# A decode layer (windowed attention plus MLP on one token): the last weight's second half loaded in three pieces, a filler matmul, and two constants made by another engine

## The chip, the cores and the metric

The kernel runs on one core of one Trainium2 chip. A core has five engines that work side by side: TensorE (PE, matmuls), VectorE (DVE), ScalarE (ACT), GpSimd (POOL) and SyncE (SP, which here only issues loads and the store), and 16 DMA engines that move data between the chip's memory (HBM) and the on-chip memory (SBUF). Matmul results go to PSUM. The metric is the device time of one execution in microseconds; the time given for a kernel is the median of its runs.

## The reference, cut to what matters

One token `x` of 1024 values is normalized; the result goes through attention over the last 4096 positions of a cache (32 query heads, 4 key/value heads, head size 128) and through an MLP, and both results are added to `x`. All inputs are bf16.

```python
xn = _layernorm(x)
# attention
q = (xn @ wq) as 32 heads of 128                 # wq 1024 x 4096
k, v = the last W = 4096 rows of k_cache, v_cache, each of 4 heads serves 8 query heads
p = softmax(q k^T * 128 ** -0.5)
A = (p v) as one row of 4096 @ wo                # wo 4096 x 1024
# MLP
h = gelu(_layernorm(xn) @ w1 + b1)               # w1 1024 x 3584
B = h @ w2 + b2                                  # w2 3584 x 1024
out = x + A + B
```

## The kernel before, in words

Every weight is used once, for one token, so the kernel is a stream of loads with the arithmetic hung beside it. In bytes: K 4 MiB, wq 8, w1 7, V 4, w2 7, wo 8.

**Loads.** SP issues nearly all of them in this order: K in four pieces (L76), wq in two halves (L85), half of b1 (L204), w1 (L207), V in four pieces (L214), w2 (L220), wo's first half, wo0, in one piece and its second half, wo1, in four (L228). A weight is laid over 128 partitions so that partition p holds consecutive rows of it; for wo, one of the two halves has 16 row groups per partition, called rows here (row r of wo1 is `tv[:, r, :]`, 128 x 1024 values, 256 KiB). ScalarE issues four small loads after its first activation (L108 to L111): x as 32 x 32 (`x32`), x and b2 as 4 x 256 each (`xb8`), and half of b1. Buffers are reused: wo1 lies where V was, so its issue waits until V has been read (L302); w2 lies where the transposed K was.

**Constants.** GpSimd makes them at the start: the zero block `zb` and identity `ident`, `zf` (512 zero columns `zeros`, the mask `sel4`, and two columns `sel01`, L112 to L120), `o8z` (128 x 32 x 3, zero, L115/L116), selection masks (L125 to L134) and `gmask`. `sel01` is a 33 x 2 matrix whose only 1 stands in row 0, column 1. ScalarE makes `ident_f`, the identity in fp32 (L96).

**Start.** `x32` is spread over the 128 partitions by four matmuls (L145), normalized twice (`layernorm`, ScalarE, TensorE and GpSimd), giving `xnT` for wq and `yT` for w1. VectorE transposes K in blocks (L191); VectorE and ScalarE move the blocks into place (L200, L202).

**Middle.** q (L237), the first MLP product (L249), scores (L266), softmax, p v (L302), and the attention row written to column 1 of `o8z` (L313), so that `o8z[:, c, 1:2]` is the vector for row c of wo, and `o8z[:, c, 0:2]` and `o8z[:, c, 1:3]` are that vector beside a zero column.

**End.** `chunk_src` lists 60 rows: 28 of w2, 16 of wo0, 16 of wo1. The first `n_bulk` = 52 (w2, wo0 and wo1's rows 0 to 7) go through two 512-column matmuls each into `accf` (L329), which had x and b2 added to it at the start (L184). Before the first row of wo0, two fp32 matmuls with zero operands clear the tail's accumulators `acct` (L326); they stand behind the last matmul of w2 by `tc.issue_after`. ScalarE copies `accf` to `bulk` (L333). The last `TAIL` = 8 rows take another way: eight short matmuls each (120 or 136 columns, L348), four side by side in the array, into the two `acct` tiles. At `idx == 0`, ahead of the first tail row, six fp32 matmuls (twelve instructions in the trace, L342) add the columns of `bulk` to the same tiles; one of their selection matrices is `sel01`. VectorE adds the rest of `bulk` while it takes the first tile (L351), ScalarE takes the second (L352), and SP and ScalarE store two rows each (L354, L355).

The order on each engine is made at build time by the framework from the order of the source, the data and its own estimate of times; `tc.issue_after(ins)` holds what is in its block behind `ins` on that engine.

Of the kernel before, what the change touches and what calls it, by code (L numbers as in the profile page):

```python
# [7 lines left out]
FP32 = mybir.dt.float32  # L8
BF16 = mybir.dt.bfloat16
ACT = mybir.ActivationFunctionType  # L10
ALU = mybir.AluOpType
# [4 lines left out]
def kernel(  # L16
# [14 lines left out]
    nc = tc.nc  # L31
    P = 128
# [13 lines left out]
    CW2 = Fd // P  # L46
    CWO = NQ // P
# [10 lines left out]
    ps_tp = ctx.enter_context(tc.tile_pool(name="ps_tp", bufs=1, space=bass.MemoryType.PSUM))  # L58
# [4 lines left out]
    def ring_tile(name):  # L63
        return ring.tile([P, RING_ELEMS], BF16, tag="ring", name=name, align_bytes=256)
# [4 lines left out]
    x_flat = A_x.rearrange("a b d -> (a b d)")  # L69
# [12 lines left out]
    for i in range(2):  # L82
# [11 lines left out]
                            pattern=[[-1, P]], channel_multiplier=1)  # L94
    ident_f = consts.tile([P, P], FP32)
# [7 lines left out]
    x32 = consts.tile([32, 32], BF16)  # L103
# [1 line left out]
    b1_8 = consts.tile([8, NH], BF16)  # L105
    b1_v = B_b1.rearrange("(a n) -> a n", a=8)
    with tc.issue_after(first_exp.ins):
        nc.scalar.dma_start(out=x32[:], in_=x_flat.rearrange("(a n) -> a n", a=32))  # L108
        nc.scalar.dma_start(out=xb8[0:4, :], in_=x_flat.rearrange("(a n) -> a n", a=4))
        nc.scalar.dma_start(out=xb8[4:8, :], in_=B_b2.rearrange("(a n) -> a n", a=4))  # L110
        nc.scalar.dma_start(out=b1_8[0:4, :], in_=b1_v[0:4, :])  # L111
    zf = consts.tile([P, 512 + Hq + 2], FP32)  # L112
    nc.gpsimd.memset(zf[:], 0.0)
    zeros = zf[:, 0:512]
    o8z = consts.tile([P, CWO, 3], BF16)  # L115
    nc.gpsimd.memset(o8z[:], 0.0)  # L116
    sel4 = zf[:, 512:512 + Hq]
    sel01 = zf[0:33, 512 + Hq:]
    nc.gpsimd.affine_select(out=sel01, in_=sel01, compare_op=ALU.not_equal, fill=1.0, base=-1,
                            pattern=[[1, 2]], channel_multiplier=2)  # L120
    qm_f = zb[:, P:P + 160]
    spread = zb[0:Hq, 288:800].rearrange("h (q p) -> h q p", q=4)
    sel_b = zb[0:8, 800:1056].rearrange("k (s m) -> k s m", s=2)
# [1 line left out]
    for sel, base in ((sel_x, 0), (sel_x, -64), (sel_b, 0)):  # L125
        nc.gpsimd.affine_select(out=sel, in_=sel, compare_op=ALU.not_equal, fill=1.0, base=base,
                                pattern=[[-16, 2], [-1, sel.shape[2]]], channel_multiplier=16)
    for R in range(4):
        nc.gpsimd.affine_select(out=sel4, in_=sel4, compare_op=ALU.not_equal, fill=1.0, base=-32 * R,
                                pattern=[[-1, Hq]], channel_multiplier=1)  # L130
# [3 lines left out]
                            pattern=[[-1, 4], [1, P]], channel_multiplier=-4)  # L134
# [4 lines left out]
                            pattern=[[-REP, Hkv]], channel_multiplier=1)  # L139
    nc.gpsimd.affine_select(out=gmask[:], in_=gmask[:], compare_op=ALU.is_ge, fill=0.0, base=REP - 1,  # L140
                            pattern=[[REP, Hkv]], channel_multiplier=-1)
# [38 lines left out]
    acch = ps_acc.tile([P, 2, 512], FP32, tag="acch", name="acch")  # L180
    for b in range(2):
        nc.scalar.copy(out=accq[:, b, :], in_=zeros)
    for s in range(2):
        nc.tensor.matmul(accf[0:64, 256 * s:256 * s + 256], lhsT=sel_x[:, s, :], rhs=xb8[:], start=(s == 0), stop=False)  # L184

# [34 lines left out]
    nc.sync.dma_start(out=w2v, in_=w2_v)  # L220
    chunk_src += [("h", r, w2v[:, r, :]) for r in range(CW2)]
    wo_v = A_wo.rearrange("(p c) n -> p c n", p=P)
    for i, cuts in enumerate([[0, 16], [0, 8, 13, 15, 16]]):
        nr = CWO // 2
        t = ring_tile(f"wo{i}")
        tv = t[:].rearrange("p (r n) -> p r n", r=nr)
        for a, b in zip(cuts[:-1], cuts[1:]):
            nc.sync.dma_start(out=tv[:, a:b, :], in_=wo_v[:, nr * i + a:nr * i + b, :])  # L228
        chunk_src += [("o", nr * i + r, tv[:, r, :]) for r in range(nr)]


    for i, w3 in enumerate(wq_tiles):
        for r in range(4):
            c = 4 * i + r
            for j in range(NJQ):
                b, t = divmod(j, 4)
                nc.tensor.matmul(accq[32 * t:32 * t + 1, b, :], lhsT=xnT[:, c:c + 1], rhs=w3[:, r, j * 512:(j + 1) * 512],  # L237
                                 start=(c == 0), stop=(c == C - 1), tile_position=(0, 32 * t))
# [6 lines left out]
    for c in range(C):  # L245
        for b in range(2):
            for t in range(4):
                j = 2 * t + b
                nc.tensor.matmul(acch[32 * t:32 * t + 1, b, :NH], lhsT=yT[:, c:c + 1], rhs=w1v[:, c, j * NH:(j + 1) * NH],  # L249
                                 start=False, stop=(c == C - 1), tile_position=(0, 32 * t))  # L250
# [11 lines left out]
    for a in range(WQ4 // 512):  # L262
        for R in range(4):
            for g in range(Hkv):
                c0 = WQ4 * R + 512 * a
                nc.tensor.matmul(sp[32 * R:32 * R + 32, a, :], lhsT=qm[:, g, :], rhs=kT[:, g, c0:c0 + 512],  # L266
                                 start=(g == 0), stop=(g == Hkv - 1), tile_position=(0, 32 * R))
# [33 lines left out]
    for c in range(NCH):  # L301
        nc.tensor.matmul(o_all[:].rearrange("h g d -> h (g d)"), lhsT=eTb[:, 32 * c:32 * c + 32], rhs=v4[:, :, c, :],  # L302
                         start=(c == 0), stop=(c == NCH - 1))
# [18 lines left out]
    for idx, (kind, c, wap) in enumerate(chunk_src[:n_bulk]):  # L322
        if idx == CW2:
            with tc.issue_after(last.ins):
                for i, (t, n) in enumerate(zip(acct, widths)):
                    nc.tensor.matmul(t[64 * i:64 * i + 34, :], lhsT=zeros[:, 0:34], rhs=zeros[:, 0:n], start=True, stop=False,  # L326
                                     tile_position=(0, 64 * i))
        for half in range(2):
            last = nc.tensor.matmul(accf[32 * half:32 * half + 1, :], lhsT=vec[kind](c),  # L329
                                    rhs=wap[:, half * 512:(half + 1) * 512],  # L330
                                    start=False, stop=(idx == n_bulk - 1), tile_position=(0, 32 * half))
# [4 lines left out]
    parts = [(i, r, half) for r in range(2) for i in range(2) for half in range(2)]  # L336
    cols = ((0, NE), (NE, 256))
    for idx, (kind, c, wap) in enumerate(chunk_src[n_bulk:]):
        if idx == 0:
            for i, r, half in [(1, 0, 0), (1, 0, 1), (0, 1, 0), (0, 1, 1), (1, 1, 0), (1, 1, 1)]:  # L340
                g0 = 64 * i + 32 * half
                nc.tensor.matmul(acct[i][g0:g0 + 2, :], lhsT=row_sel[(half, r)],  # L342
                                 rhs=bulk[0:33, 256 * r + cols[i][0]:256 * r + cols[i][1]],
                                 start=False, stop=False, tile_position=(0, g0))
        for i, r, half in parts:
            g0 = 64 * i + 32 * half
            w0 = 512 * half + 256 * r
            nc.tensor.matmul(acct[i][g0:g0 + 2, :], lhsT=o8z[:, c, 1 - r:3 - r], rhs=wap[:, w0 + cols[i][0]:w0 + cols[i][1]],  # L348
                             start=False, stop=(idx == TAIL - 1 and r == 1), tile_position=(0, g0))
# [36 lines left out]
```

## Time and profile before

| | us |
|---|---|
| median of 3 runs (101.68 to 101.92) | 101.8 |
| the profiled execution, its own time | 101.61 |
| its span, first to last instruction | 99.5 |
| PE busy | 47.6 |
| VectorE busy | 37.5 |
| ScalarE busy | 28.9 |
| GpSimd busy | 8.9 |
| bytes read from HBM | 39.86 MB |
| rate over the span | 401 GB/s |

A page of the profile gives busy time per engine, groups of instructions with what ended the idle time before them (written `[idle <-releaser]`), the chain of work that ended last, and the loads. A timeline line reads: start, duration, engine, source line, operation, tile written `<-` tiles read, shapes, count, idle time and releaser; `SPq` and `ACTq` are the issuing of loads by those engines. A line of a stretch reads: its length, then busy time and count for PE, its weight loads, VectorE, ScalarE and GpSimd, then the granted TensorE clock (1.00 is full), the DMA engines' mean busy share, and GB/s. The busy shares of 48% and less show that no engine is full over the whole span; the loads are at 94% (the queue of SP's and the other ordinary loads, as a share of the 16 DMA engines' time).

### The profile page before, as it was taken

What the parts mean: (1) busy time and instruction counts of PE and PEld (TensorE: products, weight loads), DVE (VectorE), ACT (ScalarE), POOL (GpSimd) and SP (SyncE); (2) the same over time, 40 slices, a digit from 0 to 9 for tenths busy, and PEclk for the clock granted to TensorE, in tenths of its full rate; (3) what the DMA queues carried; (4) which work ended last, traced back from release to release, by engine and by line L of the source; (5) the groups of instructions that cost most, each with busy time, mean ns of one, the idle gap of its engine ahead of it and who ended that gap; (6) DMA issues with size and microseconds to landing.
All of it is one profiled execution on the core that took longest, in us unless ns stands there. A gap on an engine that the chain in (4) does not pass through costs nothing.

```text
span 99.5 us, 1001 instructions
## 1 busy us (share of the span) xinstructions
PE 47.6 (48%) x405; PEld 20.2 (20%) x405; DVE 37.5 (38%) x25; ACT 28.9 (29%) x32; POOL 8.9 (9%) x35
## 2 busy tenths in 40 slices
PE   0005110007600880089139807999100999895770
PEld 0003110002100310063036402334000333341240
DVE  0079999999999970010613015000600000000001
ACT  5306200007999999900150080000010000000201
POOL 7921560000000000000001000000000000000000
PEclk9999999999999999999999985579955558999999
DMA  2999999999999888999499999899899999899930
GB/s 46 389 409 435 484 428 474 474 422 422 448 422 581 369 369 369 392 669 415 181 425 422 435 576 392 369 576 491 369 392 418 422 422 422 362 441 408 394 114 1
DMA packets 2539, 39.91 MB, mean 401 GB/s; under 512 B 340, under 2 KB 360, under 8 KB 616
## 3 DMA queue, kind: packets, MB, share of 16 engines
q1 hardware_dynamic: 2460, 39.85, 93.9%
q8 instruction: 3, 0.05, 0.2%
q10 hardware_dynamic: 76, 0.01, 0.1%
HBM read 39.86 MB, written 0.00 MB: 401 GB/s over the span
## 4 chain that ended last, share of the span: by engine, by line
DMA 79%; PE 14%; SPq 3%; issue 1%; DVE 0%; DVEq 0%
DMA v_sb<-in_A_v_cache_dram 32%; DMA wo<-in_A_wo_dram 25%; DMA kq<-in_A_wq_dram 17%; PE o_all L302 10%; DMA kq<-in_A_k_cache_dram 5%; PE accq L237 4%; SPq L214 1%; SPq L228 1%; SPq L207 0%; PE acct L348 0%; DVE res L351 0%; DVEq L351 0%
## 5 line engine op out<-in xcount | busy, mean ns | idle before, releaser
L200 ACT COPY kt<-kt 32x4096 bf16<-32x4096 bf16 x5 | 18.0, 3601 | 10.2 <-DVE kt L191 10.2
L191 DVE STREAM_TRANSPOSE kt<-kq 128x4096 bf16<-128x4096 bf16 x4 | 17.4, 4413 | 5.6 <-DMA kq<-in_A_k_cache_dram 5.6
L202 DVE COPY kt<-kt 32x4096 bf16<-32x4096 bf16 x11 | 13.4, 1218 | 0.2
L302 PE MATMUL o_all<-v_sb,w1t 128*32 128x512 bf16 x32 | 9.8, 480 | 3.4 <-DMA v_sb<-in_A_v_cache_dram 3.4
L329 PE MATMUL accf<-w2t 128*1 128x512 bf16 x56 | 8.9, 496 | 4.8 <-DMA w2t<-in_B_w_dram 4.8
L351 DVE TENSOR_TENSOR res<-acct,bulk 34x120 bf16<-34x120 f32 x1 | 0.3, 275 | 25.1 <-PE acct L348 25.1
L237 PE MATMUL accq<-kq,xnT 128*1 128x512 bf16 x32 | 3.6, 625 | 10.2 <-DMA kq<-in_A_wq_dram 10.2
L333 ACT COPY bulk<-accf 34x512 f32<-34x512 f32 x1 | 0.6, 579 | 20.9 <-PE accf L329 20.9
L237 PE MATMUL accq<-wq,xnT 128*1 128x512 bf16 x32 | 3.6, 627 | 6.1 <-DMA wq<-in_A_wq_dram 6.1
L329 PE MATMUL accf<-wo,o8z 128*1 128x512 bf16 x48 | 5.5, 379 | 1.6 <-DMA wo<-in_A_wo_dram 1.6
L237 PEld LDWEIGHTS <-xnT 128*1 128x1 bf16 x64 | 2.1, 115 | 20.6 <-issue 20.6
L302 PEld LDWEIGHTS <-w1t 128*32 128x32 bf16 x32 | 3.7, 117 | 9.4 <-issue 7.4
L329 PEld LDWEIGHTS <-w2t 128*1 128x1 bf16 x56 | 3.0, 103 | 10.3 <-issue 8.6
L249 PE MATMUL acch<-w1t,yT 128*1 128x448 bf16 x64 | 5.1, 488 | 0.0
L305 DVE TENSOR_TENSOR o_m<-o_all,grs 32x512 f32<-32x512 f32 x1 | 0.7, 679 | 9.1 <-PE o_all L302 9.1
L297 DVE STREAM_TRANSPOSE w2t<-w1t 128x896 bf16<-128x896 bf16 x1 | 1.7, 1702 | 6.2 <-ACT w1t L294 6.2
L145 PE MATMUL x_ps<-x,zb 32*128 32x8 bf16 x4 | 0.2, 163 | 7.9 <-DMA x<-in_A_x_dram 7.9
L309 ACT CAST o_bf<-o_f 32x128 bf16<-32x128 f32 x1 | 0.3, 297 | 12.6 <-DVE o_f L307 12.6
L266 PE MATMUL sp<-kt,zb 128*32 128x512 bf16 x32 | 3.7, 631 | 0.3 <-DVE zb L258 0.3
L253 PE MATMUL qT_ps<-zb,w1t 128*128 128x128 bf16 x8 | 1.0, 311 | 5.2 <-ACT w1t L239 5.2
L293 POOL TENSOR_SCALAR zcol<-l_loc 128x1 f32<-128x1 f32 x1 | 0.2, 238 | 36.9 <-ACT w1t L281 36.9
L249 PEld LDWEIGHTS <-yT 128*1 128x1 bf16 x64 | 3.1, 108 | 1.5
(80 smaller groups left out, 40.6 us busy)
## 6 DMA issues: line engine op xcount, KB each, us to landing
w1t<-in_B_w_dram SPq DMA_DIRECT2D x1, 7168.0 KB, 24.0
w2t<-in_B_w_dram SPq DMA_DIRECT2D x1, 7168.0 KB, 29.8
kq<-in_A_k_cache_dram SPq DMA_DIRECT2D x4, 1024.0 KB, 7.1
kq<-in_A_wq_dram SPq DMA_DIRECT2D x1, 4096.0 KB, 17.2
wq<-in_A_wq_dram SPq DMA_DIRECT2D x1, 4096.0 KB, 24.3
v_sb<-in_A_v_cache_dram SPq DMA_DIRECT2D x4, 1024.0 KB, 25.9
wo<-in_A_wo_dram SPq DMA_DIRECT2D x1, 4096.0 KB, 39.1
wo<-in_A_wo_dram SPq DMA_DIRECT2D x1, 2048.0 KB
```

Of the source, the lines that this page charges most:

```text
L191: nc.vector.transpose(out=scr[:, g, :], in_=k2[:, g, :])
L200: nc.scalar.copy(out=dst, in_=src)
L202: nc.vector.tensor_copy(out=dst, in_=src)
L214: nc.sync.dma_start(out=v4[:, g, :, :], in_=A_v_cache[0, g, Sk - W:Sk, :].rearrange("(p c) d -> p c d", p=P))
L228: nc.sync.dma_start(out=tv[:, a:b, :], in_=wo_v[:, nr * i + a:nr * i + b, :])
L237: nc.tensor.matmul(accq[32 * t:32 * t + 1, b, :], lhsT=xnT[:, c:c + 1], rhs=w3[:, r, j * 512:(j + 1) * 512], start=(c == 0), stop=(c == C ...
L249: nc.tensor.matmul(acch[32 * t:32 * t + 1, b, :NH], lhsT=yT[:, c:c + 1], rhs=w1v[:, c, j * NH:(j + 1) * NH], start=False, stop=(c == C - 1 ...
L253: nc.tensor.transpose(qT_ps[:, b * 4 + hh, :], q_sb[:, b, hh * Dh:(hh + 1) * Dh], ident)
L266: nc.tensor.matmul(sp[32 * R:32 * R + 32, a, :], lhsT=qm[:, g, :], rhs=kT[:, g, c0:c0 + 512], start=(g == 0), stop=(g == Hkv - 1), tile_po ...
L297: nc.vector.transpose(out=hT, in_=h_sb.rearrange("p (d c) -> p c d", c=CW2))
L302: nc.tensor.matmul(o_all[:].rearrange("h g d -> h (g d)"), lhsT=eTb[:, 32 * c:32 * c + 32], rhs=v4[:, :, c, :], start=(c == 0), stop=(c == ...
L329: last = nc.tensor.matmul(accf[32 * half:32 * half + 1, :], lhsT=vec[kind](c), rhs=wap[:, half * 512:(half + 1) * 512], start=False, stop= ...
```

## The change

Five edits:

- wo1 is loaded in pieces of 9, 6 and 1 rows, no longer 8, 5, 2 and 1.
- Before the first row of wo1 (`idx == CW2 + CWO // 2`, row index 44) a filler matmul is issued behind the last matmul of wo0: fp32 zeros, 33 columns of weights, 512 moving columns, into a PSUM tile that nobody reads.
- The six matmuls that add `bulk` come before the second tail row, no longer before the first; so wo1's row 8 comes ahead of them.
- `sel01` and `o8z` are no longer made by GpSimd (a masked select and a memset). ScalarE copies one column of `ident_f` into `sel01`'s second column and zeros into `o8z`.
- `x32` is loaded by two loads of 16 partitions each, no longer by one of 32.

```diff
     with tc.issue_after(first_exp.ins):
-        nc.scalar.dma_start(out=x32[:], in_=x_flat.rearrange("(a n) -> a n", a=32))
+        for a0 in (0, 16):
+            nc.scalar.dma_start(out=x32[a0:a0 + 16, :], in_=x_flat.rearrange("(a n) -> a n", a=32)[a0:a0 + 16, :])
...
     o8z = consts.tile([P, CWO, 3], BF16)
-    nc.gpsimd.memset(o8z[:], 0.0)
     sel4 = zf[:, 512:512 + Hq]
     sel01 = zf[0:33, 512 + Hq:]
-    nc.gpsimd.affine_select(out=sel01, in_=sel01, compare_op=ALU.not_equal, fill=1.0, base=-1,
-                            pattern=[[1, 2]], channel_multiplier=2)
...
     for b in range(2):
         nc.scalar.copy(out=accq[:, b, :], in_=zeros)
+    nc.scalar.copy(out=sel01[:, 1:2], in_=ident_f[0:33, 0:1])
+    nc.scalar.copy(out=o8z[:].rearrange("p c f -> p (c f)"), in_=zeros[:, 0:3 * CWO])
...
-    for i, cuts in enumerate([[0, 16], [0, 8, 13, 15, 16]]):
+    for i, cuts in enumerate([[0, 16], [0, 9, 15, 16]]):
...
+        if idx == CW2 + CWO // 2:
+            with tc.issue_after(last.ins):
+                fill = ps_tp.tile([P, 512], FP32, tag="tp", name="fill")
+                nc.tensor.matmul(fill[0:33, :], lhsT=zeros[:, 0:33], rhs=zeros, start=True, stop=True)
         for half in range(2):
             last = nc.tensor.matmul(accf[32 * half:32 * half + 1, :], lhsT=vec[kind](c),
...
     for idx, (kind, c, wap) in enumerate(chunk_src[n_bulk:]):
-        if idx == 0:
+        if idx == 1:
             for i, r, half in [(1, 0, 0), (1, 0, 1), (0, 1, 0), (0, 1, 1), (1, 1, 0), (1, 1, 1)]:
```

## The prediction

> **What bounds the kernel now.** I read the chain of waits first: does an engine or the load stream set the end?
>
> ```profile
> DMA 79%; PE 14%; SPq 3%; issue 1%; DVE 0%; DVEq 0%
> DMA v_sb<-in_A_v_cache_dram 32%; DMA wo<-in_A_wo_dram 25%; DMA kq<-in_A_wq_dram 17%; PE o_all L302 10%; DMA kq<-in_A_k_cache_dram 5%; PE accq L237 4%; SPq L214 1%; SPq L228 1%; SPq L207 0%; PE acct L348 0%; DVE res L351 0%; DVEq L351 0%
> ```
>
> The stream does: 79% of the span is loads, and 39.9 MB at a mean of 401 GB/s fill 99.5 us. Pieces in which PE or SP stands in the chain (o_all L302, SPq L228) lie in front of loads that still had others ahead of them, so they are no price. The timeline of PE at the end shows what each piece of wo's second half (wo1) costs:
>
> ```profile
> 89.73 0.81 PE L329 MATMUL accf<-wo,o8z 128*1 128x512 bf16 x6
> 91.77 1.89 PE L329 MATMUL accf<-wo,o8z 128*1 128x512 bf16 x16 [1.23 <-DMA wo<-in_A_wo_dram]
> ...
> 94.89 0.76 PE L348 MATMUL acct<-wo,o8z 128*2 128x120 bf16 x40
> 96.04 0.41 PE L348 MATMUL acct<-wo,o8z 128*2 128x120 bf16 x16 [0.38 <-DMA wo<-in_A_wo_dram]
> 96.65 0.29 PE L348 MATMUL acct<-wo,o8z 128*2 128x120 bf16 x8 [0.20 <-DMA wo<-in_A_wo_dram]
> ```
>
> PE waits for wo1's rows 0 to 7 until 91.77, for rows 13 and 14 until 96.04, for row 15 until 96.65; wo's first half started at 86.92. So eight rows take 4.85 us (0.606 each), seven rows in two pieces 4.27, the last 0.61. Behind the last landing stand 0.29 us of PE, 0.28 of VectorE and the store.
>
> Then the stream's own end, in quarter microseconds (the last two columns are the DMA engines' busy share and GB/s):
>
> ```profile
> 95.00:95.25 0.25, 0.25 (x26) 0.25 (x22) 0.00 (x0) 0.00 (x0) 0.00 (x0) 1.00 0.41 156
> 95.25:95.50 0.25, 0.25 (x28) 0.21 (x15) 0.00 (x0) 0.00 (x0) 0.00 (x0) 1.00 0.12 49
> 95.50:95.75 0.25, 0.16 (x10) 0.00 (x0) 0.00 (x0) 0.00 (x0) 0.00 (x0) 1.00 0.11 41
> ```
>
> 0.12 of 16 is two engines: the last microsecond belongs to two that lag. The page gives instruction fetches three packets and 0.2% of the engines' time, 0.002 x 16 x 99.5 / 3 = 1.1 us each, and two of them fall inside the stream (between 48.5 and 50, and 69 and 70.2 us), so I read one fetch on each laggard. The change adds no PE work before 90 us that would shift those two.
>
> Last, the clock, in stretches between the moments at which the granted clock changes (PE busy is the second number, the clock the third from the end):
>
> ```profile
> 55.55:58.96 3.41, 1.35 (x28) 0.71 (x20) 0.00 (x0) 1.94 (x2) 0.00 (x0) 1.00 1.46 625
> ...
> 69.20:72.60 3.40, 1.10 (x8) 0.50 (x7) 1.68 (x2) 0.35 (x2) 0.00 (x0) 1.00 1.06 455
> ...
> 89.67:93.08 3.41, 2.18 (x24) 0.79 (x20) 0.00 (x0) 0.00 (x0) 0.00 (x0) 1.00 0.94 399
> 93.08:96.50 3.42, 2.31 (x74) 1.16 (x71) 0.00 (x0) 0.58 (x1) 0.00 (x0) 1.00 0.63 249
> ```
>
> The changes (near 58.96, 65.78, 72.6, 82.84) lie whole multiples of 3.41 us apart. Stretches with PE busy 1.35 us (40%) and 1.10 us (32%) were followed by half clock; 2.18 (64%) and 2.31 (68%) were not. The limit lies between 40% and 64%.
>
> **The change, part by part.**
>
> *Pieces 8, 5, 2, 1 become 9, 6, 1.* One load less. With r per row and d per piece, 8r + d = 4.85 and r + d = 0.61 give d below 0.01 us; 8r + d = 4.85 and 7r + 2d = 4.27 give 0.02. The far bound: V comes in four pieces. From 32.59 (wq's second half) to 60.29 (V) is 27.70 us for w1 and V; w2, as large as w1, takes 77.27 - 60.29 = 16.98; so V takes 10.72, against 32.59 - 22.91 = 9.68 for the same bytes in one piece: 0.35 us for each of three more. That stretch holds a fetch of about 1 us, which explains it nearly whole, so I take d = 0.01 and keep 0.35. The issues (four, 1.75 us from 70.09) have wo's first half still ahead until 86.92; one of 0.43 us less saves nothing.
>
> Landings: nine rows at 91.77 + 0.61 = 92.38, rows 9 to 14 at 96.03, row 15 at 96.64. PE's work behind 96.03 grows from 24 matmuls to 56. Rate: 40 in 0.76 us, the last one 0.218 (median of L348), is (0.76 - 0.218)/39 = 13.9 ns from start to start. 56 of them end at 96.03 + 55 x 0.0139 + 0.218 = 97.01, and row 15 is in place before its turn (48 x 0.0139 = 0.67, at 96.70). Before: 96.65 + 0.29 = 96.94. So **+0.07 us**. The upper bound is the 16-group's 0.41/16 = 25.6 ns: 96.03 + 1.43 = 97.46, +0.52. I take 13.9, the longest uninterrupted group.
>
> *Row 8 ahead of the six selections of bulk.* The 16 bulk matmuls run 92.38 to 94.27 (1.89), row 8 another 0.11; ScalarE's copy to 94.89 (0.04 + 0.58), the twelve matmuls of L342 from 94.95 for 0.6 (94.34 to 94.96 now) to 95.55. The next work waits for 96.03. Cost 0; 0.48 us of cover. If the order stayed as it was, the same cover would hold it.
>
> *Filler.* L326 clears 120 and 136 columns in fp32 in 0.43 us; 512 columns are 0.86 us by that if its positions run in turn, 1.6 if side by side, 0.21 if fp32 cost as much as one 512-column bf16 matmul (two started per 0.21 in wo). From 90.54 (89.73 + 0.81) it ends between 90.75 and 92.2, before 92.38 in all cases: 0. What it buys is busy time: 89.67 to 93.08 would hold 0.87 + 0.86 + 0.70 = 2.43 us (71%), without it 1.57 (46%), inside the open interval. The poorest 3.41 us, from the filler's end at 91.40, hold 92.38 to 94.38 = 2.0 (59%); before, from 90.54, 1.89 (55%).
>
> [...]
>
> *Start.* These lines show the cover:
>
> ```profile
> 7.93 0.24 PE L145 MATMUL x_ps<-x,zb 32*128 32x8 bf16 x4 [7.93 <-DMA x<-in_A_x_dram]
> ...
> 22.91 3.58 PE L237 MATMUL accq<-kq,xnT 128*1 128x512 bf16 x32 [10.22 <-DMA kq<-in_A_wq_dram]
> ...
> 23.11 7.22 ACT L200 COPY kt<-kt 32x4096 bf16<-32x4096 bf16 x2 [10.20 <-DVE kt L191]
> ```
>
> GpSimd loses 0.17 (o8z) and 0.18 us (sel01) and its last mask comes earlier, but x_ps waits for x, not for it: 0. ScalarE gains two copies; bounds 0.17 (smallest activation) and 0.30 (L309), together under 0.6, beside 10.20 us idle: 0. The second x load adds an issue of 0.38 us (L108), so x may be complete at 8.3; xn is ready near 12.2 and wanted at 22.91: 0. If that cover were gone, it would cost those 0.4 us.
>
> [...]
>
> One thing moves with the extra load. wq's halves and b1 are issued at 5.64, 8.29 and 10.71, when K's pieces 0, 1 and 2 have landed: each waits for the eighth load before it. With one more ahead, the ScalarE-issued half of b1 waits for piece 0 (behind it the accf copy, 4.13 to about 5.7; ScalarE's next work is at 8.21), and wq's halves for pieces 1 and 2, at 8.29 and 10.71. K's last bytes are then still coming: piece 3 lands near 10.71 + 2.42 = 13.1, and a load needs about 4.83 - 2.42 = 2.4 us from issue to its first byte, so wq's first bytes are there at 10.7: some 2 us of cover. Past it, every microsecond is one at the end.
>
> **Sum.** +0.07 against the profiled execution's own 101.61 us (span 99.5 and 2.1 around it): 101.68. The median of the runs is 101.80, 0.19 higher; on it, **101.87**. A difference under 0.2% (0.2 us) can't be told from none, so my forecast is no difference, with its own range 101.67 to 102.0.
>
> **Rivals.**
>
> 1. A piece costs more than two landings show. At 0.35 us the sum is -0.35 + 0.08 = -0.27: 101.53. For it: V's time. Against: the one-row piece at 0.61. [...] 0.12.
> 2. Some of the runs shown already lose the clock at the end. The stretch at 55% is inside the open interval, and an execution whose 3.41 us steps fall there runs the last work at half clock: bulk's selections 0.62 more, the 40 about 0.55 more, less 0.58 idle, then 0.1 to 0.3 on the last rows, some 0.4 us at most. The filler raises that stretch to 59%. Worth about 0.25 on the median: 101.55. Against: the runs spread by 0.24 only. 0.10.
> 3. **Slower: the clock falls in front of the last 56 matmuls.** If the filler (on zeros) doesn't count as busy, the stretch to 93.08 holds 46%; if the limit is above that, PE gets half clock from there to the end: 96.03 + 55 x 0.0278 + 0.3 = 97.86 instead of 96.94, +0.9: 102.7. Against: nothing shows that it doesn't count. 0.13.
> 4. Slower: the long group starts at the 16-group's pace, +0.5: 102.3. Against: the 40-group at 13.9. 0.11.
> 5. Slower: the stream starves when wq waits for a later piece of K, or a fetch moves; 0.4 to 1.0. Against: 2 us of cover. 0.08.
> 6. The order written isn't the order built (row 8 behind the selections): no change to the sum; it is within the forecast.
>
> **How the numbers follow.** No difference 0.46; faster 0.12 + 0.10 = 0.22; slower 0.13 + 0.11 + 0.08 = 0.32. The range takes in rivals 1, 2 and 4, from 101.48 to 102.4; outside are rival 3, part of 5 and little else, under 0.2.
>
> **What would show it.** In the timeline after: PE's waits for wo end near 92.4 and 96.0 and none ends at row 15 (one group of 56 of about 0.98 us); filler done before 92.2; granted clock 1.00 from 83 us to the end; L342 over before 96; SP's first wq issue near 8.3. Wrong is the forecast if the last landing moves by over 0.2 us, if the group of 56 takes over 1.2 us, or if the clock drops after 90 us.

## The result, and the profile after

The changed kernel takes 101.47 us (median of 14 runs, 101.30 to 101.80) against 101.84 us (14 runs, 101.68 to 101.96): ratio 0.9968, 95% interval 0.9958 to 0.9978. It is faster by 0.3%, a small difference but clear of the noise. The forecast was 101.87 and no difference, with a range of 101.48 to 102.4 that takes in three of the rivals.

The profiled execution of the changed kernel took 101.56 us, and its span is 99.8 us, *longer* than the 99.5 of before. So the gain is not in the span. First the two lines of its chain of waits:

```profile
DMA 80%; PE 13%; SPq 2%; issue 1%; DVE 0%; DVEq 0%
DMA v_sb<-in_A_v_cache_dram 32%; DMA wo<-in_A_wo_dram 27%; DMA kq<-in_A_wq_dram 14%; PE o_all L302 9%; DMA kq<-in_A_k_cache_dram 7%; PE accq L237 4%; SPq L214 1%; PE acct L352 1%; SPq L76 0%; SPq L207 0%; SPq L228 0%; DVE res L355 0%; DVEq L355 0%
```

The stream of loads sets the span as before. The timeline of PE at the end (L331 is the filler, L333, L346 and L352 were L329, L342 and L348):

```profile
87.16 3.62 PE L333 MATMUL accf<-wo,o8z 128*1 128x512 bf16 x32 [1.21 <-DMA wo<-in_A_wo_dram]
90.70 1.05 PE L331 MATMUL fill<-zf 128*33 128x512 f32 x2
92.59 1.46 PE L333 MATMUL accf<-wo,o8z 128*1 128x512 bf16 x12 [0.84 <-DMA wo<-in_A_wo_dram]
...
94.31 0.27 PE L352 MATMUL acct<-wo,o8z 128*2 128x120 bf16 x4
95.15 0.28 PE L346 MATMUL acct<-bulk,ident_f 33*2 33x136 f32 x2 [0.57 <-ACT bulk L337]
...
96.23 1.00 PE L352 MATMUL acct<-wo,o8z 128*2 128x120 bf16 x56 [0.45 <-DMA wo<-in_A_wo_dram]
```

Nine rows arrive 5.43 us after wo0 started (92.59 - 87.16), six more 3.64 us later: 0.60 to 0.61 us per row again. The filler is over at 91.75, the selections start at 95.15 and are done half a microsecond ahead of 96.23, and one group of 56 takes 1.00 us.

The last microsecond again has a DMA share of two engines or less (stretches of a quarter microsecond, columns as before):

```profile
95.25:95.50 0.25, 0.25 (x11) 0.18 (x5) 0.00 (x0) 0.00 (x0) 0.00 (x0) 1.00 0.12 49
95.50:95.75 0.25, 0.25 (x8) 0.04 (x1) 0.00 (x0) 0.00 (x0) 0.00 (x0) 1.00 0.04 16
95.75:96.00 0.25, 0.03 (x2) 0.04 (x1) 0.00 (x0) 0.00 (x0) 0.00 (x0) 1.00 0.13 49
```

The clock at the end, in stretches between this execution's own steps of 3.41 us (its clock changes at 71.12, 81.36 and 98.43):

```profile
88.19:91.60 3.41, 3.41 (x26) 1.02 (x22) 0.00 (x0) 0.00 (x0) 0.00 (x0) 1.00 0.96 411
91.60:95.01 3.41, 2.15 (x25) 0.88 (x24) 0.00 (x0) 0.49 (x1) 0.00 (x0) 1.00 0.94 392
95.01:98.43 3.42, 1.63 (x68) 1.16 (x68) 0.28 (x1) 0.36 (x2) 0.00 (x0) 1.00 0.06 22
```

The clock is full up to 98.43, past the last matmul (96.23 + 1.00), with PE busy 100%, 63% and 48%; it halves after the last of these. At the start, the timeline shows the moved work under its cover:

```profile
8.20 0.24 PE L143 MATMUL x_ps<-x,zb 32*128 32x8 bf16 x4 [8.20 <-DMA x<-in_A_x_dram]
...
8.29 0.33 SPq L85 DMA_DIRECT2D kq<-in_A_wq_dram  x1
...
23.05 3.60 ACT L200 COPY kt<-kt 32x4096 bf16<-32x4096 bf16 x1 [9.88 <-DVE kt L191]
```

x_ps is 0.27 us later, wq's first half is issued at 8.29 in place of 5.64, ScalarE still idles 9.88 us. None of this reaches the end.

Where, then, is the gain? Time less span is 101.61 - 99.5 = 2.11 us before and 101.56 - 99.8 = 1.76 after. The record of the granted clock runs on behind the last instruction; a stretch of the profile shows half clock to the end of that record and 1.00 behind it. Before:

```profile
101.00:102.00 1.00, 0.00 (x0) 0.00 (x0) 0.00 (x0) 0.00 (x0) 0.00 (x0) 0.54 0.00 0
```

After:

```profile
101.00:102.00 1.00, 0.00 (x0) 0.00 (x0) 0.00 (x0) 0.00 (x0) 0.00 (x0) 0.57 0.00 0
```

0.54 is half clock for 0.92 us and 0.57 for 0.86, so the record ends at 101.92 and at 101.86, in both 0.3 us past the execution's own time (101.61, 101.56). In all 20 profiled executions of this document that distance is 0.30 or 0.31 us, which suggests that what lies in front of the span is the same in all. What is left between the last instruction and that end is 2.4 us before and 2.1 after. The 0.35 us sit *behind* the last recorded instruction.

### The profile page after: what moved, and what is told of

Read it like the earlier page. It is cut to its first block, busy times and chain, and to the rows that moved or that the text cites. A ratio compares the mean times of both kernels' runs of the same rounds, so it can differ in the third digit from the quotient of the medians.

```text
span 99.8 us, 1004 instructions
## 1 busy us (share of the span) xinstructions
PE 47.3 (47%) x407; PEld 20.3 (20%) x407; DVE 37.5 (38%) x25; ACT 29.1 (29%) x34; POOL 8.6 (9%) x33
## 4 chain that ended last, share of the span: by engine, by line
DMA 80%; PE 13%; SPq 2%; issue 1%; DVE 0%; DVEq 0%
DMA v_sb<-in_A_v_cache_dram 32%; DMA wo<-in_A_wo_dram 27%; DMA kq<-in_A_wq_dram 14%; PE o_all L302 9%; DMA kq<-in_A_k_cache_dram 7%; PE accq L237 4%; SPq L214 1%; PE acct L352 1%; SPq L76 0%; SPq L207 0%; SPq L228 0%; DVE res L355 0%; DVEq L355 0%
## 5 line engine op out<-in xcount | busy, mean ns | idle before, releaser
L333 PE MATMUL accf<-w2t 128*1 128x512 bf16 x56 | 8.1, 460 | 6.0 <-DMA w2t<-in_B_w_dram 6.0
L302 PE MATMUL o_all<-v_sb,w1t 128*32 128x512 bf16 x32 | 8.8, 443 | 2.6 <-DMA v_sb<-in_A_v_cache_dram 2.6
L333 PE MATMUL accf<-wo,o8z 128*1 128x512 bf16 x48 | 5.5, 379 | 2.0 <-DMA wo<-in_A_wo_dram 2.0
L249 PE MATMUL acch<-w1t,yT 128*1 128x448 bf16 x64 | 6.2, 574 | 0.0
L333 PEld LDWEIGHTS <-w2t 128*1 128x1 bf16 x56 | 2.8, 97 | 10.9 <-issue 8.6
L249 PEld LDWEIGHTS <-yT 128*1 128x1 bf16 x64 | 3.6, 122 | 1.8
```

## The experiments

The reading in all of them is the time, the ratio to the kernel before, and time less span. "Length" is the number of instructions that the trace records for GpSimd, with its semaphore and register instructions; it is 60 before and 57 after. The expectations of e7 to e10 count the entries of GpSimd's list as it is built, which are fewer: 40 before, 38 after. Spans are given to 0.1 us, so a single time less span is good to 0.05.

| run | what it is | length | time, us | ratio [95%] | time less span, median (range) |
|---|---|---|---|---|---|
| e0 | before, unchanged | 60 | 101.74 | 0.999 [0.998, 1.000] | 2.12 (2.05 to 2.24) |
| e1 | x in two loads | 60 | 101.93 | 1.0001 [0.9992, 1.0010] | 2.14 (2.09 to 2.22) |
| e2 | constants on ScalarE | 57 | 101.47 | 0.9966 [0.9955, 0.9977] | 1.79 (1.68 to 1.90) |
| e3 | pieces, filler, order | 60 | 101.83 | 0.9994 [0.9984, 1.0004] | 2.12 (2.07 to 2.26) |
| after | all | 57 | 101.47 | 0.9968 [0.9958, 0.9978] | 1.72 (1.67 to 1.88) |
| e4 | o8z alone moved | 59 | 101.70 | 0.9992 [0.9980, 1.0004] | 1.99 (1.92 to 2.02) |
| e5 | sel01 alone moved | 58 | 101.45 | 0.9967 [0.9949, 0.9986] | 1.75 (1.70 to 1.79) |
| e6 | both on VectorE | 57 | 101.43 | 0.9956 [0.9945, 0.9967] | 1.78 (1.71 to 1.87) |
| e7 | e2 and 3 idle clears | 60 | 101.86 | 1.0012 [1.0000, 1.0023] | 2.14 (2.08 to 2.25) |
| e8 | before and 3 idle clears | 63 | 101.56 | 0.9969 [0.9959, 0.9979] | 1.86 (1.84 to 1.90) |
| e9 | before and 9 | 69 | 101.92 | 1.0013 [1.0003, 1.0023] | 1.78 (1.74 to 1.89), span 100.1 |
| e10 | after, 3 clears more off GpSimd | 54 | 101.45 | 0.9964 [0.9950, 0.9978] | 1.76 (1.74 to 1.87) |
| e11 | after without filler | 57 | 101.54 | 0.9976 [0.9966, 0.9986] | 1.77 (1.68 to 1.85) |
| e12 | before and 24 | 84 | 101.39 | 0.9964 [0.9952, 0.9975] | 1.71 (1.68 to 1.86) |
| e13 | before and 60 | 120 | 101.46 | 0.9965 [0.9953, 0.9977] | 1.76 (1.67 to 1.84) |
| e14 | before and 32 | 92 | 101.38 | 0.9955 [0.9936, 0.9975] | 1.73 (1.68 to 1.78) |
| e15 | before and 64 | 124 | 101.47 | 0.9969 [0.9953, 0.9984] | 1.73 (1.67 to 1.77) |
| e16 | before and 128 | 188 | 101.78 | 0.9990 [0.9963, 1.0017] | 2.05 (2.00 to 2.09) |
| e17 | before and 137 | 197 | 101.91 (one run) | | 1.81, span 100.1 |

### Which edit: e0 to e3

e0 is the kernel before with a comment line. e1 has only this edit:

```diff
-        nc.scalar.dma_start(out=x32[:], in_=x_flat.rearrange("(a n) -> a n", a=32))
+        for a0 in (0, 16):
+            nc.scalar.dma_start(out=x32[a0:a0 + 16, :], in_=x_flat.rearrange("(a n) -> a n", a=32)[a0:a0 + 16, :])
```

e2 has only the edits of `o8z` and `sel01`, e3 only the pieces, the filler and `idx == 1`, each as in the diff of the change.

> The kernel before, unchanged (a comment line is added), to learn how its time and its span stand to each other over many executions. In the profiled executions the time less the span is 2.11 us before and 1.76 us after (1.67 to 1.88 over 14). Theory A (the gain lies outside the span): time less span is near 2.1 in nearly all executions here, and spans are near 99.7, no longer than those of the changed kernel. Theory B (the profiled execution of before was one with a short span by chance, and the gain is in the stream of loads): time less span is near 1.75 here too, and spans are near 100.1. Ratio to before 1.000 within 0.001 by both.

> Only the x load in two halves. Theory A1 (this edit makes the gain, through the order of waits of the first loads): ratio near 0.997, time less span near 1.75. Theory A2 (another edit does): ratio 1.000, time less span near 2.1. Theory B (stream's end): ratio 1.000, since the end is untouched. By all: SP issues wq's first half near 8.3 us, no longer 5.6, and x_ps starts near 8.2.

> Only the two constants moved from GpSimd to ScalarE. Theory A1: ratio 1.000. Theory A2 (the number of GpSimd instructions sets something outside the span): ratio near 0.997, time less span near 1.75. Theory B: 1.000.

> Only the end: pieces of 9, 6 and 1 rows, the filler, the selections of bulk behind row 8. Theory B: the whole gain is here, ratio near 0.997, last wait for wo earlier by some 0.3 us. Theory A1: ratio 1.000 to 1.001 (the longer group of 56 costs 0.05 to 0.1 us). Theory A3 (number of loads or of TensorE instructions sets something outside the span): ratio near 0.997 with time less span near 1.75.

e2 is as fast as the whole change, e1 and e3 are no different from before. e0 shows that the long stretch behind the span is no accident of one profile: 2.05 to 2.24 in 12 executions, and the 34 of the kernel before on the same chip lie between 2.05 and 2.26; the two groups (2.05 and up, 1.90 and down) don't overlap. Theory B is out, and so are A1 (e1) and A3 (e3); A2 remained.

### What of the two constants: e4 to e7

e4 moves `o8z` alone, e5 `sel01` alone. e6 gives both to VectorE, e7 is e2 with idle work on GpSimd:

```diff
-    nc.gpsimd.memset(o8z[:], 0.0)
+    nc.vector.memset(o8z[:], 0.0)
...
+    nc.vector.tensor_copy(out=sel01[:, 1:2], in_=ident_f[0:33, 0:1])
```

```diff
     nc.gpsimd.memset(mhalf[:], -0.5)
+    pad = consts.tile([P, 1], FP32, name="pad")
+    for _ in range(3):
+        nc.gpsimd.memset(pad[:], 0.0)
```

> Only o8z is made by ScalarE; sel01 stays on GpSimd (one GpSimd instruction less, one ScalarE instruction more). Read: time less span, 2.05 to 2.26 in the kernels with GpSimd's full list so far, 1.67 to 1.90 in those with the shorter. Theory C (what GpSimd has to run sets a stretch outside the span, in proportion): about 1.95, halfway. Theory C2 (the length of GpSimd's list matters as a step): either 2.1 or 1.75, not between. Theory D (ScalarE's added copies do it): as C. Theory E (the odd 33-partition select does it): 2.1.

> Only sel01 is made by ScalarE; o8z stays on GpSimd. Time less span: theory C about 1.95; C2 either 2.1 or 1.75; D as C; E 1.75.

> Both constants made by VectorE in place of ScalarE, so GpSimd's list is as short as after the change and ScalarE's is that of before. Time less span: theories C and C2 1.75 and a time near 101.5; D 2.1 and 101.85; E 1.75.

> Both constants on ScalarE, and three clears of one unused column added on GpSimd, so that its list is one longer than before the change (41 against 40 in the order of instructions). Time less span: C and C2 2.1 and a time near 101.85; D 1.75 and 101.5; E 1.75 and 101.5.

ScalarE has nothing to do with it (e6), and three idle clears give the 0.35 us back (e7): the number of GpSimd's instructions counts, not what they compute. e5, on its own, has the whole gain. e4 shortens the stretch behind the span by about a third of it (1.99), which can't be told from none in its time. The step lies between lengths 58 and 60.

### Is it the length? e8 to e10, and the filler, e11

e8 and e9 add 3 and 9 clears to the kernel before, in the way of e7. e10 makes `ones_f`, `zf` and `gmask`'s first clear on VectorE in the changed kernel. e11 leaves the filler out.

> The kernel before with three clears of an unused column added on GpSimd (43 entries in its list against 40 before and 38 after the change). Time less span: it was 2.12 at 40 entries, 2.14 at 41, 1.99 or 1.75 at 39, 1.75 to 1.79 at 38. Theory C (in proportion to the length): 2.3 to 2.6. Theory C2 (a step that lies between 38 and 40 entries): 2.1 to 2.2, as at 41.

> The kernel before with nine such clears on GpSimd (49 entries). Time less span: theory C (in proportion) 3 us or more; theory C2 (one step) 2.1 to 2.2. If the step is one of a series with a period, this tells whether the next one lies within nine entries.

> The changed kernel with three more of GpSimd's clears (ones_f, zf, gmask) made by VectorE, which is idle until 5.6 us; GpSimd's list has 35 entries. Time less span: theory C 1.3 to 1.5 and a time near 101.1, ratio 0.993; theory C2 1.7 to 1.8 and a time near 101.47, ratio 0.997, since everything these clears feed is covered by 10 us.

> The changed kernel without the filler matmul. PE then waits from about 90.7 to 92.5 us with nothing to do. Theory F (the filler keeps the clock): in some executions the granted clock falls to half in front of the last 56 matmuls, which then take about 1.8 us in place of 1.0; ratio between 0.997 and 1.006, with a wider spread of times. Theory G (no need of it): ratio 0.996 to 0.997 and the same spread as with it.

Both theories of length fell: 63 is short again, against C and C2 alike, and at 69 the stretch behind the span is short but the span itself is 0.4 longer. That run shows the cost in the open. In the list of SP's waits, the line of SP's last instruction waiting at the closing barrier (total, times, longest) is, before:

```profile
SPq L381 <- PEq L381: 0.6, 2, 0.4
```

with 69 instructions on GpSimd (e9; its last line is L384):

```profile
SPq L384 <- PEq L384: 0.9, 2, 0.8
```

The waits name PE, but the late one is GpSimd: its last two recorded instructions start 0.43 us apart (99.55 and 99.98), in every shorter list 0.08 (99.31 and 99.39 before). So GpSimd pauses for 0.35 us between its 68th and 69th instruction. A load of instructions follows, 0.70 us after the last of them starts; it stands in e9's DMA view of the time from 98.9 us on, where the kernel before has no packet at all:

```profile
DMA packets 1, 0.01 MB, mean 2 GB/s; under 512 B 0, under 2 KB 0, under 8 KB 0
...
q14 instruction: 1, 0.01, 0.5%
```

Its record is 8192 bytes. I formed theory H from this: GpSimd pauses for about 0.35 us at a fixed place of its list, behind the 68th recorded instruction; what that costs depends on what waits behind it.

e11 answers another question. Without the filler PE waits 1.83 us:

```profile
92.63 1.46 PE L329 MATMUL accf<-wo,o8z 128*1 128x512 bf16 x12 [1.83 <-DMA wo<-in_A_wo_dram]
...
96.28 1.00 PE L348 MATMUL acct<-wo,o8z 128*2 128x120 bf16 x56 [0.45 <-DMA wo<-in_A_wo_dram]
```

The 56 matmuls take 1.00 us as with it, and the ten times spread as with the filler (101.38 to 101.81, and 101.30 to 101.80). The ratios overlap. No run shows the filler to be of use. In this profile of e11 the poorest stretch before the end holds 2.07 us of PE work (61%); the 46% that the prediction worked out for another position of the steps was not met in it, so the filler's use in such an execution stays open.

### A place or a length: e12 to e17

All add clears to the kernel before as in e7, with 24, 60, 32, 64, 128 and 137 in the range.

> The kernel before with 24 clears of an unused column added on GpSimd (84 recorded GpSimd instructions; 60 before, 57 after the change, 69 with nine clears). With 69 the trace has a pause of 0.43 us in place of 0.08 between GpSimd's last two instructions, and the time behind the span is short again. Theory H (GpSimd pauses about 0.35 us at a fixed place of its list, behind the 68th recorded instruction; where that place falls behind the last wait of the kernel it is paid, where it falls in front of one it is hidden): here the place lies in front of the 84 - 16 = 68th or so, among the instructions that wait for the middle of the kernel, so the pause is hidden: time less span 1.7 to 1.9, span 99.7, time near 101.47, ratio 0.996 to 0.997, although the kernel only does more. Theory I (the length of the list costs, by some other rule): 101.85 or more.

> As before with 60 such clears (120 recorded GpSimd instructions), most of them back to back between 5.5 and 10 us. Theory H: the trace shows one pause of about 0.35 us among the clears, at the 68th or 69th recorded instruction, and the end is as short as in the changed kernel unless a second such place, 64 further on, falls on the end: 68 + 64 = 132 is 12 behind the last of 120, about where the list of 57 stands to 69, so time less span 1.7 to 1.9. Theory I: no pause at that place.

The kernel that only does more work is the faster one: 84 instructions, 101.39 us. The load of instructions has moved into the middle; e12's DMA view of 9 to 12 us has the line

```profile
q14 instruction: 1, 0.01, 0.6%
```

and the kernel before has none there. A pause is not to be seen at the new place. In e12 the 68th and 69th instructions start 0.478 us apart, and the same pair of instructions in the kernel before 0.479. So one part of the expectation failed: e13 shows no pause among its clears either (they follow each other at 0.157 us through the 68th and 69th), though the load of instructions is there, at 10 to 11 us. Theory H takes the pause to be hidden there; no run shows that it takes place at all in the middle.

> The kernel before with 32 idle clears on GpSimd (92 recorded GpSimd instructions). Known so far of the time less span: short (1.70 to 1.79) at 54, 57, 58, 84 and 120 recorded instructions, 1.99 at 59, 2.12 at 60, 1.86 at 63, and at 69 a pause of 0.35 us inside the span. Theory J (the place that pauses comes back at a fixed distance along the list, and is exposed only where GpSimd runs short instructions at the end): with a distance of 32 or 16, 2.1 here and a time near 101.85; with 64 or more, 1.70 to 1.79 and 101.45. Theory K (what matters is only where the end of the list lies in some larger unit, once): 1.70 to 1.79.

> The kernel before with 64 idle clears on GpSimd (124 recorded). Theory J with a distance of 64 (or 32, 16): time less span 2.1, time near 101.85, although 120 recorded instructions gave 1.76 and 101.46. With a larger distance, or theory K: 1.70 to 1.79 and 101.45.

> The kernel before with 128 idle clears on GpSimd (188 recorded). 128 clears of 0.157 us are 20 us, which delay the normalized token to some 27 us, so the first matmuls of wq start late; the middle may move, and only the time less span is read. Theory J with a distance of 128, 64, 32 or 16: 2.1. Otherwise 1.70 to 1.79.

> The kernel before with 137 idle clears on GpSimd (197 recorded, 128 more than the list of 69 that showed the pause inside the span). Only GpSimd's last instructions are read. Theory J with a distance of 128: between the last two recorded GpSimd instructions about 0.43 us in place of 0.08, as with 69, and time less span 1.7 to 1.9. If the 2.05 us of the list of 188 had another cause: 0.08 us there.

92 and 124 are short, 188 is long again (2.00 to 2.09 in eight executions; its times spread from 101.32 to 102.39 and are not used, since with so many clears q's first matmul waits for them, in e17 for 8.7 us), and 197 shows the pause inside the span as 69 did (e17, same line of SP's waits):

```profile
SPq L384 <- PEq L384: 0.9, 2, 0.7
```

There GpSimd's last two instructions are 0.39 us apart. So both readings came back with 128 instructions more: a time less span of 2.12 us at 60 and 2.05 at 188, the pause at 69 and 197. The loads of instructions change with the length too. Once the kernel runs, the profiles show none of 8192 bytes in any list of 63 or fewer, one in each of 69 to 188, and in 197 a second one, at 101.02 us. In the lists of 84 to 124 no cost is to be seen: the medians of their time less span are 1.71 to 1.76. In those of 69 and 197, where the pause falls on the closing barrier, it is 0.35 and 0.31 us (0.43 and 0.39 less 0.08). With 60 and 188 the trace shows neither the pause nor a load behind the span. That the same pause costs the 0.35 us there is inferred from the size and from the distance of 128.

What fixes the place (behind the 68th recorded instruction, and again 128 further on) can't be read. Nor is it shown which instruction behind the span waits for GpSimd; the lengths at which the cost appears (1.99 us at 59, 2.12 at 60, 1.86 at 63) suggest that one does, and with 58 or fewer (1.72 to 1.79) none of it is to be seen.

No version beat the changed kernel by a measurable amount: the best medians (101.38 and 101.39, e14 and e12) and e6's 101.43 have intervals that overlap with its own.

## Why the prediction was wrong, point by point

**The step that failed** is in the sum: "+0.07 against the profiled execution's own 101.61 us (span 99.5 and 2.1 around it)". The 2.1 us were carried over as a constant. They went to 1.72 (median of 14). Together with it failed "GpSimd loses 0.17 (o8z) and 0.18 us (sel01) ... 0": right as time on GpSimd, whose masks are covered, but with two instructions and a semaphore instruction less (57 recorded in place of 60) the stretch behind the span was 0.35 us shorter. The price was -0.35 us in place of 0, and none of the rivals had it. With 1.72 us in place of the 2.12 that e0 measured, the sum would have been 101.87 - 0.40 = 101.47, the measured time, so nothing else in the sum has to move. Rival 1 had nearly the size (-0.27) by a mechanism that the runs refute.

**Pieces.** Right. Row time 0.606 and no cost per piece worked out to landings 5.46 and 3.65 us apart (92.38 - 86.92, 96.03 - 92.38); measured 5.43 and 3.64. Rival 1 (0.35 us per piece) would have shown in e3, whose ratio is 0.9994 [0.9984, 1.0004], at most 0.16 us.

**The group of 56.** Right in the trace: forecast 0.98 us from the landing on, measured 1.00 (also in e11), and the pace of the 16-group (rival 4, 1.43) is out. The +0.07 us is too small to be seen in the times; e3's interval is -0.16 to +0.04 us, so it may be a little less.

**Filler.** Its place was right (done at 91.75, bounds 90.75 to 92.2), its length mis-sized: 1.05 us by the timeline, 0.86 forecast; it lay under the wait all the same. Rival 3 (clock lost in front of the 56) didn't come, not even without the filler in the execution profiled. The loss itself does occur. In e7, which has no filler and the end of the kernel before, the clock halved at 96.83, and the last eight matmuls took 0.40 us in place of 0.29. Rival 2 (a gain because before loses the clock at the end) is out as the cause: e2 has the whole gain without a filler, e3 none with it.

**Row 8 ahead of the selections.** The order built put row 8's matmuls among the last bulk matmuls and not behind them; the bulk copy started at 94.52 (0.2 later than worked out), and 0.45 us of wait were left in front of 96.23. No cost, as forecast.

**Start.** Right in each time: x_ps 8.20 (forecast up to 8.3), first wq issue 8.29, ScalarE's b1 issue and accf copy held to 5.6 and 5.9; no effect (e1: 1.0001).

**The clock's limit.** Reading a limit between 40% and 64% of PE's busy time from four stretches was too quick. In e2 the clock stayed full after a stretch of 43%; in e7 it halved after one of 63%:

```profile
67.88:71.30 3.42, 1.48 (x7) 0.57 (x6) 1.69 (x2) 0.08 (x1) 0.00 (x0) 1.00 0.95 407
71.30:74.72 3.42, 0.25 (x4) 0.22 (x4) 0.00 (x0) 0.43 (x2) 0.00 (x0) 1.00 0.89 386
```

```profile
93.42:96.83 3.41, 2.14 (x72) 1.09 (x69) 0.00 (x0) 0.58 (x1) 0.00 (x0) 1.00 0.54 215
96.83:98.00 1.17, 0.40 (x8) 0.10 (x7) 0.27 (x1) 0.27 (x1) 0.00 (x0) 0.50 0.00 0
```

So the busy share that the profile gives doesn't decide it alone, and what does is open.

**The laggards.** A share of 0.12, two engines' worth, stands at the stream's end after the change as before. The prediction laid it to one instruction fetch on each of the two; no run shows that.

## What to carry to other kernels

Compare time less span before believing that a change of 0.3% in a kernel of 100 us is in the schedule that the trace shows: it is one subtraction, and here it separated two groups of executions without overlap. If it differs, vary the length of each engine's instruction list with idle instructions: this kernel got faster by 0.36% with 24 useless clears on GpSimd. And a prediction should not carry the stretch around the span as a constant when an edit changes the number of GpSimd's instructions: it was 2.12 us with 60 recorded (e0) and 1.72 with 57 (after).

## What the runs showed of the hardware that was not expected

- GpSimd's last two recorded instructions start 0.43 us apart with 69 recorded (e9) and 0.39 with 197 (e17), in place of 0.08: a pause of 0.35 and 0.31 us, at lists that are 128 instructions apart. A load of 8192 bytes of instructions starts 0.70 us after the last of them in e9, and one at 101.02 us in e17. In the middle no pause is to be seen (0.478 us between the 68th and 69th in e12, 0.479 between the same two before; 0.157 in e13).
- Half clock for TensorE followed 3.41 us stretches with PE busy 40% (before), 48% (after) and 63% (e7), and didn't follow stretches of 43% (e2) and 61% (e11). No single share of busy time parts them.
